# Dilated sliding attention into a gated unit: q and k loaded for two batches in full tiles, stores in pairs from another queue

## The chip, the cores and the metric

The kernel runs on one core of a Trainium2 chip. Its engines work side by side, each through its own list of instructions, and wait for each other by semaphores: TensorE (PE in the profile; PEld is its loading of weights) multiplies into PSUM, a memory of 8 banks; VectorE (DVE) and ScalarE (ACT) read and write PSUM and the on-chip memory SBUF; GpSimd (POOL) works on SBUF alone; SyncE (SP) only issues transfers. Transfers (DMAs) are moved by 16 DMA engines that all queues share. An engine that issues a transfer does so in its place in its own list. The metric is the device time of one execution in microseconds (us), as the median of the runs.

## The reference

Eight batches, eight heads, 576 positions, 64 values per head; all inputs are float32. Each head attends to 32 earlier positions: heads 0 to 3 to the last 32 in a row ("plain"), heads 4 to 7 to every fourth of the last 128 ("dilated"). The heads' outputs, side by side, are the x of a gated unit: a causal depthwise convolution of 5 taps and a sigmoid make the gate, x @ w_val the value, and their product goes through w_out.

```python
scores = scale * np.matmul(q, k.transpose(0, 1, 3, 2))
mask_plain = (rel >= 0) & (rel < window)                                   # window 32
mask_dil = (rel >= 0) & (rel < window * dilation) & (rel % dilation == 0)  # dilation 4
masks = [mask_plain if h < H // 2 else mask_dil for h in range(H)]
attn = softmax(np.where(masks, scores, -1e9))
x = np.matmul(attn, v)                      # then (B, S, H * D)
gate_pre[s] = sum(conv_w[j] * x[s - 4 + j] for j in range(5))
out = (sigmoid(gate_pre) * (x @ w_val)) @ w_out
```

## The kernel before, in words

The unit of attention work is an "attend": two neighbouring heads of one batch, 32 in all, four per batch (`order`, line 209). Of the group numbers g, 0 and 1 are plain and 2 and 3 dilated.

**Loads** (`load`, line 304), all issued by SP. q and k of an attend are one tile each of 96 partitions and 768 float32 (288 KB): dilated, 12 positions per partition, both heads one after the other; plain, 6 positions of each head side by side. v comes as two tiles of 96 and 80 partitions when dilated (lines 330, 332) and as three transfers when plain (lines 335 and 339), in blocks of 128 positions that overlap. Six buffers of q and of k, four of plain v and three of dilated v let loads run ahead.

**One attend** (`attend`, line 472). Plain q and k are first cast to bf16 on GpSimd (lines 486, 489); dilated ones are read as the upper halves of float32. TensorE transposes six slices of 96 partitions each (lines 351 and 356, with an identity as the moving operand), and ScalarE or VectorE copies the 576 columns out of PSUM to qT and kT (lines 362 and 364). Scores are computed in two halves (line 400), each followed by an exp on ScalarE (line 403). VectorE multiplies by a mask of zeros and ones (line 408). TensorE multiplies with v and a column of ones (lines 417, 427, 431), VectorE takes the reciprocal of the sums and scales (lines 436 and 437), TensorE transposes back (lines 454 and 458), and the result is copied to xT (362 or 364), which holds all eight batches.

**The gated unit** (`gated`, line 590) of a batch follows its four attends: for each of four chunks of 128 channels 20 convolution matmuls on halves of the array (line 547), a tanh on ScalarE (line 599, a sigmoid up to scale), eight value matmuls (line 557, which need all four attends' xT), and one VectorE instruction that forms y (line 603). Then come four output tiles of 128 positions, four matmuls each (line 565), copied out by ScalarE or VectorE (lines 570 and 572). Each is stored at once by SP (line 617, 256 KB). The last 32 positions of each half, of four batches together, make two more tiles after batches 3 and 7, stored by line 624. A second copy of w_val and w_out with head halves swapped serves the second half of the positions.

**The order** of every engine's list is worked out by a planner ahead of the run (`Plan`, lines 34 to 126). A task has dependencies, a cost on each engine that could do it, a priority and the PSUM banks it needs. The planner steps through a modelled time, takes the task that could start earliest (among close ones, the one of lowest priority number), and assigns its engine and banks. Its model lets at most eight transfers be in flight when SP issues one (`FLIGHT`), and runs all transfers one after the other:

```python
dma_free = max(dma_free, est + c + 1.3) + nbytes / rate
t.end = dma_free + 0.5
```

The planned order is then emitted, and semaphores keep the data right, however far the chip is from the model. Stores and loads share SP's list, so a store whose tile is not ready holds the loads behind it.

Of the kernel before, what the change touches and what calls it, by code (L numbers as in the profile page):

```python
# [33 lines left out]
class Plan:  # L34
# [6 lines left out]
    FLIGHT = 8  # L41

# [8 lines left out]
    def run(self):  # L51
        for t in self.tasks:
            t.deps = [d() if callable(d) else d for d in t.deps]
            t.deps = [d for d in t.deps if d is not None]
        free = {e: 0.9 for e in self.OVER}
# [6 lines left out]
        while todo:  # L62
            best = {}
            for t in todo:
                ready = 0.0
                for d in t.deps:
# [3 lines left out]
                    ready = max(ready, d.end + self.SYNC[src])  # L70
# [37 lines left out]
            if t.lag:  # L108
                free[e] = est + c
                nbytes, rate = t.lag  # L110
                dma_free = max(dma_free, est + c + 1.3) + nbytes / rate
                t.end = dma_free + 0.5
                flight.append(t.end)
            else:
                t.end = est + c
                free[e] = t.end - self.OVER[e]
# [13 lines left out]
def kernel(  # L130
# [10 lines left out]
    nc = tc.nc  # L141
# [32 lines left out]
    NQ, NV, NET, NX, NO = 6, 4, 3, 3, 6  # L174
    NY = 3
    qs = bufs(NQ, [96, 2 * S * D // 96], FP32, "q")
    ks = bufs(NQ, [96, 2 * S * D // 96], FP32, "k")
    vps = bufs(NV, [128, NB, 2, DA], FP32, "vp")
    vas = bufs(3, [96, 2, R * D], FP32, "va")
    vzs = bufs(3, [80, 2, R * D], FP32, "vz")  # L180
    vd0 = bufs(3, [96, 2, R, DA], BF16, "vda")
    vd1 = bufs(3, [80, 2, R, DA], BF16, "vdb")
    qcs = bufs(3, [96, 6, 2, D], BF16, "qc")
    kcs = bufs(3, [96, 6, 2, D], BF16, "kc")
    qTs = bufs(3, [128, S], BF16, "qT")
    kTp = bufs(3, [128, 32 + S], BF16, "kTp")
    kTd = bufs(3, [128, 640], BF16, "kTd")
# [5 lines left out]
    osbs = bufs(NO, [128, Dm], FP32, "osb")  # L193
    xT = consts.tile([128, NCH, B * SB], BF16, name="xT")
# [14 lines left out]
    order = [(b, g) for b in range(B) for g in ((2, 0, 3, 1) if b == 0 else (0, 2, 1, 3))]  # L209
# [7 lines left out]
    nth = {}  # L217
    seen = {True: 0, False: 0}
    for i in range(N):
        nth[i] = seen[is_dil(i)]  # L220
        seen[is_dil(i)] += 1
# [19 lines left out]
    def c_mask_p():  # L241
        band(mask_p[:, 0:96].rearrange("p (j t) -> p j t", j=6), 32, [[1, 6], [6, 16]], 1)
# [10 lines left out]

    def c_ident2():
# [4 lines left out]
    def c_kd():  # L259
        for x in kTd:  # L260
            nc.vector.memset(x[:, S:640], 0.0)
# [4 lines left out]

    def c_kp():
        for x in kTp:
            nc.vector.memset(x[:, 0:32], 0.0)
# [5 lines left out]
    def c_vp():  # L275
        for x in vps:
            nc.gpsimd.memset(x[:, :, :, D:DA], 1.0 - 2.0 ** -9)
            nc.gpsimd.memset(x[0:32, 0, :, :], 0.0)

    def c_xpad():  # L280
        nc.vector.memset(xT.rearrange("z c (b t) -> z c b t", b=B, t=SB)[:, :, :, 0:4], 0.0)
# [4 lines left out]
    K_kp = add("kp", -7, {"DVE": 0.2}, lambda t: c_kp())  # L286
# [6 lines left out]
    K_sp = add("sp", -5, {"DVE": 1.2}, lambda t: spread(mask_p, 12), [K_mp])  # L293
# [3 lines left out]
    LD = {}  # L297
    PAIR = {}

    def ld(name, i, nbytes, rate, emit, deps):  # L300
        t = add(name, i, {"SP": 0.45}, emit, list(deps), lag=(nbytes, rate))
        return t

    def load(i):
        b, g = order[i]
        dil = is_dil(i)
        def was(m, nm):
            return lambda: PAIR.get(m, {}).get(nm)

        qt, kt = qs[i % NQ], ks[i % NQ]  # L310
        P = PAIR[i] = {}
        for nm, dst, src, dep in (("q", qt, q, was(i - NQ, "rq")), ("k", kt, k, was(i - NQ, "rk"))):
            two = src[b, 2 * g:2 * g + 2]
            if dil:
                s = two.rearrange("h (p r) d -> (h p) (r d)", r=12)
                d = dst
            else:
                s = two.rearrange("h (p r) d -> p h (r d)", r=6)
                d = dst.rearrange("p (h c) -> p h c", h=2)
# [386 lines left out]
```

## Time and profile before

| | |
|---|---|
| median of 3 runs | 277.98 us (276.61 to 279.22) |
| the profiled execution | 276.3 us, of which its span (first to last instruction) is 274.3 |
| mean granted TensorE clock | 0.869 |
| busy: TensorE, VectorE, ScalarE, GpSimd | 190.6, 120.7, 118.4, 58.3 us |
| moved by DMA | 42.09 MB, 153 GB/s over the span |
| loads of q and k | 64 of 288 KB, 6.6 and 7.0 us to landing (median) |
| stores | 36 of 256 KB, 2.1 us to landing (median) |

How to read the profile: "busy" is the time in which an engine executes, as a share of the span in brackets. "40 slices" cuts the span into equal pieces; each digit is the busy share in tenths. "The chain that ended last" goes back from the last instruction, step by step, to what released it, and gives each engine's and line's share; a long wait that is not on it costs nothing. A row of a group reads: line, engine, operation, output<-input, count, busy time and mean of one, and after the bar the idle time before it with the releaser. A row of waits reads: who waited, for whom, total us, times, longest. A row of the timeline begins with its start and length in us. A row of a stretch gives its limits and length, the busy time of TensorE, its weight loads, VectorE, ScalarE and GpSimd with counts, then the clock, the DMA share (in sums of overlapping transfers it can pass 1) and GB/s.

### The profile page before, as it was taken

What the parts mean: (1) busy time and instruction counts of PE and PEld (TensorE: products, weight loads), DVE (VectorE), ACT (ScalarE), POOL (GpSimd) and SP (SyncE); (2) the same over time, 40 slices, a digit from 0 to 9 for tenths busy, and PEclk for the clock granted to TensorE, in tenths of its full rate; (3) what the DMA queues carried; (4) which work ended last, traced back from release to release, by engine and by line L of the source; (5) the groups of instructions that cost most, each with busy time, mean ns of one, the idle gap of its engine ahead of it and who ended that gap; (6) DMA issues with size and microseconds to landing.
All of it is one profiled execution on the core that took longest, in us unless ns stands there. A gap on an engine that the chain in (4) does not pass through costs nothing.

```text
span 274.3 us, 6193 instructions
## 1 busy us (share of the span) xinstructions
PE 190.6 (69%) x2548; PEld 131.0 (48%) x2548; DVE 120.7 (44%) x213; ACT 118.4 (43%) x196; POOL 58.3 (21%) x104
## 2 busy tenths in 40 slices
PE   3667567858678658587585778787887577677860
PEld 2556444544454446345454535555665345544520
DVE  5645444524445423514624355454674334535400
ACT  3453313652464551055430446455844352663150
POOL 6453210404021310070040510034050600100000
PEclk9999999977997955959759579999779799979995
DMA  7999991195974599305899017788999240003041
GB/s 194 244 238 259 252 217 39 51 247 146 240 137 148 163 245 234 66 0 167 217 224 182 3 38 213 212 215 271 236 217 224 54 155 0 26 17 115 2 158 71
DMA packets 47093, 42.09 MB, mean 153 GB/s; under 512 B 26453, under 2 KB 39253, under 8 KB 47066
## 3 DMA queue, kind: packets, MB, share of 16 engines
q1 hardware_dynamic: 46000, 40.64, 61.0%
q0 software_dynamic: 1056, 1.05, 2.3%
q8 instruction: 20, 0.33, 0.5%
q14 instruction: 7, 0.06, 0.1%
q10 hardware_dynamic: 10, 0.01, 0.0%
HBM read 32.78 MB, written 9.44 MB: 154 GB/s over the span
## 4 chain that ended last, share of the span: by engine, by line
PE 55%; DVE 20%; ACT 15%; issue 4%; DMA 2%; SPq 1%; POOL 0%; ACTq 0%; DVEq 0%
PE ps L557 13%; PE ps L565 11%; PE ps L547 10%; ACT et L403 8%; DVE xn L437 6%; DVE y L603 6%; PE ps L400 5%; PE ps L351 3%; ACT gate L599 3%; PE ps L356 3%; PE ps L417 3%; DVE xm L437 3%; DVE rec L436 2%; PE ps L454 2%; DMA q<-in_q_dram 2%
## 5 line engine op out<-in xcount | busy, mean ns | idle before, releaser
L403 ACT ACTIVATE et<-ps 128x576 bf16<-128x576 f32 x64 | 39.9, 650 | 38.8 <-PE ps L400 17.1
L557 PE MATMUL ps<-xT,w_val 128*128 128x288 bf16 x256 | 42.5, 317 | 7.3 <-DVE xn L437 2.5
L565 PE MATMUL ps<-w_out,y 128*128 128x512 bf16 x128 | 38.5, 438 | 3.5 <-DVE xm L437 1.2
L547 PE MATMUL ps<-xT,conv_d 64*64 64x288 bf16 x640 | 34.1, 344 | 8.1 <-ACT et L403 5.8
L603 DVE SCALAR_TENSOR_TENSOR y<-gate,ps 128x576 bf16<-128x576 bf16 x32 | 23.8, 752 | 30.1 <-PE ps L557 19.9
L557 PEld LDWEIGHTS <-w_val 128*128 128x128 bf16 x256 | 26.4, 108 | 18.4 <-issue 10.0
L570 ACT ACTIVATE osb<-ps 128x512 f32<-128x512 f32 x34 | 20.3, 597 | 23.5 <-PE ps L565 22.9
L599 ACT ACTIVATE gate<-ps 128x576 bf16<-128x576 f32 x32 | 20.6, 652 | 22.1 <-PE ps L547 10.4
L436 DVE RECIPROCAL rec<-ps 96x8 f32<-96x8 f32 (+1 forms) x48 | 10.0, 209 | 45.2 <-ACT gate L599 6.9
L547 PEld LDWEIGHTS <-conv_d 64*64 64x64 bf16 x640 | 21.5, 125 | 13.6 <-issue 9.3
L609 POOL COPY y_rem<-y 128x256 bf16<-128x256 bf16 x8 | 3.6, 456 | 110.8 <-DVE y L603 108.4
L437 DVE TENSOR_TENSOR xn<-ps,rec 96x512 bf16<-96x512 f32 (+1 forms) x32 | 26.2, 820 | 1.1
L516 POOL CAST vda<-va 96x512 bf16<-96x512 f32 x16 | 11.4, 710 | 57.1 <-DMA va<-in_v_dram 52.4
L565 PEld LDWEIGHTS <-y 128*128 128x128 bf16 x128 | 12.4, 108 | 18.8 <-issue 10.8
L362 ACT COPY xT<-ps 128x576 bf16<-128x576 bf16 x20 | 12.8, 639 | 19.3 <-PE ps L458 15.6
L408 DVE TENSOR_TENSOR et<-et,mask_p 128x1152 bf16<-128x1152 bf16 x16 | 13.4, 840 | 17.4 <-ACT et L403 17.4
L362 ACT COPY qT<-ps 128x576 bf16<-128x576 bf16 x19 | 12.2, 642 | 17.1 <-DVE xm L437 5.8
L364 DVE COPY xT<-ps 128x576 bf16<-128x576 bf16 x12 | 9.1, 757 | 18.5 <-PE ps L454 8.5
L489 POOL CAST kc<-k 96x768 bf16<-96x768 f32 x16 | 13.8, 861 | 15.7 <-DMA k<-in_k_dram 15.6
L408 DVE TENSOR_TENSOR et<-et,mask_d 128x1152 bf16<-128x1152 bf16 x15 | 12.5, 836 | 9.2 <-ACT et L403 9.2
L400 PE MATMUL ps<-qT,kTd 64*128 64x96 bf16 (+1 forms) x256 | 10.0, 209 | 9.0 <-DVE xn L437 2.7
L400 PE MATMUL ps<-qT,kTp 64*128 64x96 bf16 x192 | 9.6, 234 | 8.2 <-DVE xn L437 4.6
(67 smaller groups left out, 242.1 us busy)
## 6 DMA issues: line engine op xcount, KB each, us to landing
q<-in_q_dram SPq DMA_DIRECT2D x32, 288.0 KB, 6.6
k<-in_k_dram SPq DMA_DIRECT2D x32, 288.0 KB, 7.0
out_dram<-osb SPq DMA_DIRECT2D x36, 256.0 KB, 2.1
vp<-in_v_dram SPq DMA_DIRECT2D x32, 160.0 KB, 6.8
va<-in_v_dram SPq DMA_DIRECT2D x16, 192.0 KB, 5.8
vz<-in_v_dram SPq DMA_DIRECT2D x16, 160.0 KB, 7.3
vp<-in_v_dram SPq DMA_DIRECT2D x16, 48.0 KB, 7.0
w_val<-in_moe_w_val_dram POOLq DMA_DIRECT2D x1, 512.0 KB, 11.2
```

The lines of the kernel that those rows point to most:

```text
L362: nc.scalar.copy(out=out_, in_=in_)
L400: nc.tensor.matmul(out=o, lhsT=l, rhs=r, start=True, stop=True)
L403: nc.scalar.activation(out=et[:, hf * 576:hf * 576 + 576].rearrange("p (b c) -> p b c", b=2), in_=ps[:, :, 0:HALF], func=AF.Exp, scale=scale)
L408: eng.tensor_tensor(out=et[:, 0:ET], in0=et[:, 0:ET], in1=(mask_d if is_dil(i) else mask_p)[:, 0:ET], op=ALU.mult)
L436: nc.vector.reciprocal(out=rec[:, :, 0:n], in_=av[:, :, :, D])
L437: nc.vector.tensor_tensor(out=xo, in0=av[:, :, :, 0:D], in1=rec[:, :, 0:n, None].to_broadcast([96, 2, n, D]), op=ALU.mult)
L547: nc.tensor.matmul(out=ps[ob:ob + D, half, 0:HALF], lhsT=conv_d[x * D:x * D + D, c, kk, :], rhs=xT[x * D:x * D + D, c, s:s + HALF], start= ...
L557: nc.tensor.matmul(out=ps[:, half, 0:HALF], lhsT=w_val[half][:, mc, c * 128:(c + 1) * 128], rhs=xT[:, mc, s:s + HALF], start=(mc == 0), st ...
L565: nc.tensor.matmul(out=ps[:, :], lhsT=cols(c), rhs=w_out[half][:, c, :], start=(c == 0), stop=(c == NCH - 1))
L570: nc.scalar.activation(out=osb, in_=ps, func=AF.Copy, scale=0.5)
L599: th = add("tanh", base + 1.0 + 0.5 * c, {"ACT": 0.66}, lambda t, cv=cv, gt=gt: nc.scalar.activation(out=gt, in_=banks(cv, 2)[:, :, 0:HALF ...
L603: y = add("y", base + 1.2 + 0.5 * c, {"DVE": 0.76}, lambda t, c=c, vl=vl, gt=gt: nc.vector.scalar_tensor_tensor(out=y_all[:, c, b % NY, :] ...
```

## The change

*q and k.* Two batches form a pair. The 384 partition rows of one kind (plain or dilated), of q or k, are cut into three tiles u = 0, 1, 2 of 128 partitions (`rows`, `unit`). Tile 0 lies in the first batch and tile 2 in the second; tile 1 takes its first 64 rows from one and its last 64 from the other, which its DRAM pattern writes as a leading dimension of 2. Plain heads are now paired 0 with 2 and 1 with 3, so that 128 partitions hold two heads side by side; tile 1 of the plain kind is loaded in two pieces, one per head of the pair. `prepare` casts, transposes (128 columns a slice) and copies out 768 columns to a qT and kT that span both batches. An attend waits for the tiles that it needs: in the first batch, tile 0, and for its second attend of a kind also tile 1; in the second, tiles 1 and 2, and then tile 2.

*Stores.* Two output tiles share one buffer and go out in one transfer of 512 KB, issued by ScalarE; the two remainder tiles are evicted into one buffer and stored by two transfers, also from ScalarE.

*Weights.* With the new pairing, rows and columns of w_val, conv_w and w_out are put in order by three transfers in place of one, and both copies of w_val are formed by eight copies from a raw one that is held in w_out's second buffer until then.

*Planner and buffers.* Every dependency gets 0.1 us of slack; a task that needs a PSUM bank also waits, in the plan, for what the task that frees the bank waits for; the value matmuls wait for the convolution of their chunk; transfers from queues other than SP's are modelled otherwise; many rates and costs are changed. Batches take groups 2, 0, 3, 1 in turn. Buffers: three plain and two dilated v, two y, five batches of xT, four double output tiles. The plain mask has a first block of its own, and kT no leading zeros.

```diff
+    SLACK = 0.1
...
+        for t in self.tasks:
+            for u in t.frees:
+                u.deps += [d for d in t.deps if d not in t.frees and not d.frees]
...
-                    ready = max(ready, d.end + self.SYNC[src])
+                    ready = max(ready, d.end + self.SYNC[src] + self.SLACK)
...
-                dma_free = max(dma_free, est + c + 1.3) + nbytes / rate
-                t.end = dma_free + 0.5
+                if e == "SP":
+                    dma_free = max(dma_free, est + c + 1.3) + nbytes / rate
+                    t.end = dma_free + 0.5
+                else:
+                    dma_free = max(dma_free, est + c) + nbytes / rate
+                    t.end = est + c + 1.8 + 2 * nbytes / rate
                 flight.append(t.end)
...
-    NQ, NV, NET, NX, NO = 6, 4, 3, 3, 6
-    NY = 3
-    qs = bufs(NQ, [96, 2 * S * D // 96], FP32, "q")
-    ks = bufs(NQ, [96, 2 * S * D // 96], FP32, "k")
+    NQ, NV, NVD, NET, NX, NO, NY, NXT = 6, 3, 2, 3, 3, 4, 2, 5
+    G = 2 * NG * (S // 12)
+    qs = bufs(NQ, [128, 768], FP32, "q")
+    ks = bufs(NQ, [128, 768], FP32, "k")
...
-    vas = bufs(3, [96, 2, R * D], FP32, "va")
-    vzs = bufs(3, [80, 2, R * D], FP32, "vz")
...
-    qTs = bufs(3, [128, S], BF16, "qT")
-    kTp = bufs(3, [128, 32 + S], BF16, "kTp")
-    kTd = bufs(3, [128, 640], BF16, "kTd")
+    vas = bufs(NVD, [96, 2, R * D], FP32, "va")
+    vzs = bufs(NVD, [80, 2, R * D], FP32, "vz")
+    qcs = bufs(2, [128, 6, 2, D], BF16, "qc")
+    kcs = bufs(2, [128, 6, 2, D], BF16, "kc")
+    qTs = {kind: bufs(2, [128, 6, G], BF16, "qT" + kind) for kind in "dp"}
+    kTs = {kind: bufs(2, [128, 6 * G + 64 * (kind == "d")], BF16, "kT" + kind) for kind in "dp"}
...
-    osbs = bufs(NO, [128, Dm], FP32, "osb")
-    xT = consts.tile([128, NCH, B * SB], BF16, name="xT")
+    osbs = bufs(NO, [128, 2, Dm], FP32, "osb")
+    xT = consts.tile([128, NCH, NXT * SB], BF16, name="xT")
...
-    order = [(b, g) for b in range(B) for g in ((2, 0, 3, 1) if b == 0 else (0, 2, 1, 3))]
+    order = [(b, g) for b in range(B) for g in (2, 0, 3, 1)]
...
+    def heads(i):
+        b, g = order[i]
+        return (2 * g, 2 * g + 1) if is_dil(i) else (g, g + 2)
...
+    def rows(kind, u):
+
+        r = 12 if kind == "d" else 6
+        if u == 0:
+            part, off = [[r * D, 128]], 0
+        elif u == 1:
+            step = H * S * D - 128 * r * D
+            part, off = [[step, 2], [r * D, 64]], 128 * r * D
+        else:
+            part, off = [[r * D, 128]], H * S * D + 64 * r * D
+        width = r * D
+        if kind == "d":
+            return [(0, width, off, part + [[1, width]])]
+        if u == 1:
+            return [(x * width, width, off + x * 2 * S * D, part + [[1, width]]) for x in range(2)]
+        return [(0, 2 * width, off, part + [[2 * S * D, 2], [1, width]])]
+
+    def load_rows(src, kind, n, u, piece, dst):
+        o, w, off, ap = piece
+        base = src.offset + (2 * n * H + (NG if kind == "d" else 0)) * S * D
+        nc.sync.dma_start(out=dst[:, o:o + w], in_=bass.AP(tensor=src.tensor, offset=base + off, ap=ap))
+
+    def unit(n, kind):
+        for u in range(3):
+            first = 8 * n + (0, 2, 4)[u] + (kind == "p")
+            for w, (nm, ring, src) in enumerate((("q", qs, q), ("k", ks, k))):
+                m = SEQ.index((n, kind, u))
+                dst = ring[m % NQ]
+                before = SEQ[m - NQ] if m >= NQ else None
+                UNIT[n, kind, u, nm] = {}
+                UNIT[n, kind, u, nm]["buf"] = dst
+                pieces = rows(kind, u)
+                UNIT[n, kind, u, nm]["ld"] = [ld(
+                    "ld" + nm, first + 0.1 * w, 393.0 / len(pieces), 330.0,
+                    lambda t, dst=dst, src=src, u=u, piece=piece: load_rows(src, kind, n, u, piece, dst),
+                    [lambda before=before, nm=nm: UNIT[before + (nm,)]["free"] if before else None])
+                    for piece in pieces]
+
+    SEQ = [(n, kind, u) for n in range(B // 2) for u in range(3) for kind in "dp"]
...
+    def prepare(n, kind, u):
+
+        prio = 8 * n + (0, 2, 4)[u] + (kind == "p")
+        for nm in "qk":
+            U = UNIT[n, kind, u, nm]
+            src, got = U["buf"], U["ld"]
+            dst = (qTs if nm == "q" else kTs)[kind][n % 2]
+            m = SEQ.index((n, kind, u)) // 2
+            if kind == "p":
+                c = (qcs if nm == "q" else kcs)[m % 2]
+                before = SEQ[2 * (m - 2) + 1] if m >= 2 else None
+                raw = src
+                got = U["cast"] = add("cast", prio - 0.3, {"POOL": 0.87}, lambda t, raw=raw, c=c: nc.gpsimd.tensor_copy(
+                    c.rearrange("p j h d -> p h j d"), raw.rearrange("p (h j d) -> p h j d", h=2, j=6)),
+                    got + [UNIT[before + (nm,)]["tr"] if before else None])
+                got = [got]
+                U["free"] = U["cast"]
+                src = c
+            tr = U["tr"] = add("tr", prio - 0.05, {"PE": 0.34}, lambda t, src=src: transpose_in(t, kind, src),
+                               got + [K_ident], banks=1, mode="full")
+            if kind == "d":
+                U["free"] = tr
+            old = [PAIR[i]["sc"] for i in range(8 * (n - 2), 8 * (n - 1)) if is_dil(i) == (kind == "d")] if n >= 2 else []
+            if nm == "q":
+                U["ev"] = add("evq", prio - 0.04, {"DVE": 0.56, "ACT": 0.81}, lambda t, tr=tr, dst=dst: copy(
+                    t, dst[:, :, 128 * u:128 * u + 128], bank(tr, BF16)[:, 0:768].rearrange("p (f g) -> p f g", f=6)),
+                    [tr] + old, frees=[tr])
+            else:
+                U["ev"] = add("evk", prio - 0.04, {"ACT": 0.81, "DVE": 0.96}, lambda t, tr=tr, dst=dst: evict_k(
+                    t, kind, bank(tr, BF16), dst, u), [tr, K_kd] + old, frees=[tr])
...
+        b, g = order[i]
+        kind = "d" if dil else "p"
+        n = b // 2
+        if dil:
+            need = {(0, 2): (0,), (0, 3): (0, 1), (1, 2): (1, 2), (1, 3): (2,)}[b % 2, g]
+        else:
+            need = {(0, 0): (0,), (0, 1): (0, 1), (1, 0): (1, 2), (1, 1): (2,)}[b % 2, g]
+        ready = [UNIT[n, kind, u, nm]["ev"] for u in need for nm in "qk"]
+        qT, kT = qTs[kind][n % 2], kTs[kind][n % 2]
...
+    def out_tiles(prio, tiles, store):
...
-        sts = [add("st", prio, {"SP": 0.45}, lambda t, e=e: e(osb), [oe], lag=(nb, 340.0)) for e, nb in store]
...
+        oes, ots = [], []
+        for x, (half, cols, deps) in enumerate(tiles):
+            ot = add("ot", prio + 0.5 * x, {"PE": 0.87}, lambda t, half=half, cols=cols: outp(t, half, cols),
+                     list(deps) + K_wo[half], banks=1, mode="full")
+            oes.append(add("oe", prio + 0.5 * x, {"ACT": 0.60, "DVE": 0.69}, lambda t, x=x, ot=ot: evict_o(t, bank(ot), osb[:, x, :]),
+                           [ot] + (out_st[n - NO] if n >= NO else []), frees=[ot]))
+            ots.append(ot)
+        out_st.append([add("st", prio + 0.5, {"ACT": 0.40}, lambda t, e=e: e(osb), oes, lag=(nb, 340.0)) for e, nb in store])
+        return ots
...
-            for n in range(2):
-                t0 = half * HALF + n * 128
-                YO[b].append(out_tile(base + 3.2 + 0.5 * (2 * half + n), half,
-                         lambda c, t0=t0: y_all[:, c, b % NY, t0:t0 + 128], ys,
-                         [(lambda osb, t0=t0: nc.sync.dma_start(out=out[b, t0:t0 + 128, :], in_=osb), 262.0)]))
+            t0 = half * HALF
+            YO[b] += out_tiles(base + 3.2 + half, [
+                (half, lambda c, o=t0 + 128 * n: y_all[:, c, b % NY, o:o + 128], ys) for n in range(2)],
+                [(lambda osb, t0=t0: nc.scalar.dma_start(
+                    out=out[b, t0:t0 + 256, :].rearrange("(n p) d -> p n d", n=2), in_=osb), 524.0)])
...
     def load_w(t, dst, src):
-        nc.gpsimd.dma_start(out=dst, in_=src.rearrange("(c p) n -> p c n", p=128))
-
-    def swap_val(t):
-        wv = [w.rearrange("p m (c x d) -> p (m c) x d", x=2, d=D) for w in w_val]
+        cut = CH * 128
+        top = src[0:cut].rearrange("(x c d) n -> x d c n", x=2, c=CH)
         for x in range(2):
-            copy(t, wv[1][:, :, x, :], wv[0][:, :, 1 - x, :])
+            nc.gpsimd.dma_start(out=dst[x * D:x * D + D, 0:CH, :], in_=top[x])
+        nc.gpsimd.dma_start(out=dst[:, CH:, :], in_=src[cut:].rearrange("(c p) n -> p c n", p=128))
+
+    def order_val(t, half, part):
+        cut = CH * 128
+        raw = w_out[1]
+        lo, hi, src = ((0, cut, "p m (x c d) -> p m x c d"), (cut, Dm, "p m (c x d) -> p m x c d"))[part]
+        kw = {"x": 2, "d": D}
+        dv = w_val[half][:, :, lo:hi].rearrange("p m (c x d) -> p m x c d", **kw)
+        sv = raw[:, :, lo:hi].rearrange(src, **kw)
...
+    wv = add("ldwv", 1.0, {"POOL": 2.6}, lambda t: load_w(t, w_out[1], moe_w_val),
+             [UNIT[0, "p", 1, "q"]["ld"][0]], lag=(1049.0, 330.0))
+    K_wv = [add("ordv", 3.0 + half, {"DVE": 0.8, "ACT": 1.2}, lambda t, half=half, part=part: order_val(t, half, part),
+                [wv]) for half in range(2) for part in range(2)]
+    wo = add("ldwo", 5.0, {"POOL": 2.6}, lambda t: load_w(t, w_out[0], moe_w_out),
+             [PAIR[4]["lv"][0]], lag=(1049.0, 330.0))
+    so = [add("swo", 6.0, {"SP": 0.45}, lambda t, x=x: swap_out(t, x), [wo] + K_wv, lag=(262.0, 300.0)) for x in range(2)]
```

## The prediction

> **What bounds the kernel now.** I read the page first: busy times, the slices, the chain that ended last. In the fence: busy time by engine, the DMA row of the slices, and the chain by engine and by line.
>
> ```profile
> PE 190.6 (69%) x2548; PEld 131.0 (48%) x2548; DVE 120.7 (44%) x213; ACT 118.4 (43%) x196; POOL 58.3 (21%) x104
> ...
> DMA  7999991195974599305899017788999240003041
> ...
> PE 55%; DVE 20%; ACT 15%; issue 4%; DMA 2%; SPq 1%; POOL 0%; ACTq 0%; DVEq 0%
> PE ps L557 13%; PE ps L565 11%; PE ps L547 10%; ACT et L403 8%; DVE xn L437 6%; DVE y L603 6%; PE ps L400 5%; PE ps L351 3%; ACT gate L599 3%; PE ps L356 3%; PE ps L417 3%; DVE xm L437 3%; DVE rec L436 2%; PE ps L454 2%; DMA q<-in_q_dram 2%
> ```
>
> No engine is full. The chain hops between TensorE, VectorE and ScalarE; DMA is 2% of it, one load at the start. The slices say where that could change: the DMA engines are full for the first 39 us, then have gaps. So the second view is the busy time by stretch for 8 to 39 us, and the third the DMA alone in the kernel's last 5 us, when TensorE is done.
>
> ```profile
> 8.00:39.00 31.00, 20.74 (x288) 16.59 (x289) 15.96 (x27) 11.83 (x20) 11.45 (x14) 1.00 1.17 242
> ```
> ```profile
> 264.75 1.41 SPq L624 DMA_DIRECT2D out_dram<-osb  x2
> ```
> ```profile
> DMA  1131410222222232222223131322223132222312
> ...
> DMA packets 232, 0.46 MB, mean 93 GB/s; under 512 B 5, under 2 KB 5, under 8 KB 232
> ...
> q1 hardware_dynamic: 232, 0.46, 25.4%
> ```
>
> The last columns of the first fence are clock, DMA share and GB/s: 242 GB/s with the engines saturated, 15.1 GB/s for each of 16. The next fence, from the timeline, shows the two remainder stores (line 624) issued together, and the last is the DMA view from 267.5 to 272.5 us: their 256 KB each are still moving, with 25.4% of 16 engines busy, 4.06 engines, at 93/4.06 = 22.9 GB/s each. Their address pattern in DRAM starts with a dimension of 4 (four batches). The 2.1 us stores and the other loads start with 80, 96 or 128 rows. I read: **the leading dimension of the address pattern limits how many engines a transfer gets**, and two such transfers share the same ones, since two in flight hold four and not eight.
>
> Fourth, the first batch in the timeline and in the chain in order of time:
>
> ```profile
> 22.04 0.82 POOL L489 CAST kc<-k 96x768 bf16<-96x768 f32 x1 [0.48 <-DMA k<-in_k_dram]
> ```
> ```profile
> 39.03 2.08 PE ps L557 x8
> ...
> 254.09 2.73 PE ps L557 x21
> ```
>
> The k of attend 3, the last head pair of batch 0, is cast at 22.0; batch 0's first value matmul runs at 39.0, 17 us later, batch 7's at 254.1. So a batch takes 215.1/7 = 30.7 us, two batches 61.5, and from batch 7's first value matmul to the end it is 20.2 us. Last, the waits of SP's queue:
>
> ```profile
> SPq L617 <- ACT osb L570: 125.6, 28, 17.2
> SPq L321 <- DMA k<-in_k_dram: 8.5, 11, 1.1
> ```
>
> SP stands 125.6 us at stores whose tile is not evicted yet, with loads queued behind; and loads wait for earlier loads to land, so only a few may be in flight (the planner's FLIGHT says 8).
>
> **The change, part by part.** The sum is made on the profiled execution: 276.3 us, of which 274.3 are its span and 2.0 lie around it. It is 1.7 under the median of 277.98, and I add that at the end.
>
> *The middle tile of each triple.* Two batches' q of one kind are three tiles of 128 rows. The first and last lie in one batch. The second takes 64 rows of each, and its pattern starts with `[step, 2]`. By the remainder stores' row it runs on two engines, always the same two. Bounds: sixteen engines (a load may not follow the rule that a store follows) to two; I take two, the only row with a small leading dimension. Each such tile is 393,216 B, 196,608 per engine: 8.6 us at the 22.9 of the tail, 13.0 at the 15.1 of the saturated stretch. I take 8.6, since the other fourteen engines will mostly stand idle, as in the tail. q and k of both kinds: 34.3 us per pair of batches on those two engines (ends 34.3 and 52.1).
>
> Everything else is spread over sixteen: 42.09 MB, less 16 x 0.393 = 6.29 for the middle tiles, plus 0.26 for the plain v's wider first block (64 for 48 KB), 36.06 MB, 2.25 per engine. At 22.9 that is 98 us, at 15.1 149; I take 20 GB/s, nearer the tail's row: 113, or 28.2 per pair. The remainder stores stay on four engines, these two among them: 0.197 MB more than their even share, 8.6 us, 2.1 per pair. Sum **64.6 us per pair** (60.9 to 91).
>
> The Trainium skill, "DMA: Bandwidth & Descriptors", section "Why a DMA increments its semaphore by 16 and not by 1", speaks against this change: the engine count is the largest number up to 16 that divides the slowest dimension of both sides, and the lowest-numbered engines are taken. The four-engine tail agrees; which engines they are no view here names. By its other rule, in "Rules for kernel authors" (128 partitions for bandwidth), the tiles would gain and the sum would be the fast rival's 271.
>
> *Start.* Ahead of the last middle tile, in the planner's priority order, go four u=0 tiles (98 KB per engine) and the v of attends 0 to 2 (70 KB): 168 KB at the start's 15.1, 11.1 us. With 2.5 us to the first data and 34.3, k for attend 3 is ready at 48 in place of 22, 26 us late. From that cast to batch 0's last xT copy was 12 us (33.43 to 34.2), so its value matmuls can't start before 60: 21 late. Between, some conv and the next pair's transposes can be brought forward, but the next tiles stand behind in the same queues. I take **+17** (12 to 26).
>
> *After the start.* The engines' 64.6 stands against compute's 61.5, less 1.8 from the savings below, 59.7: 4.9 late per pair, three more pairs, **+15** (+4 to +94). The loads may run a pair ahead (six buffers), which makes the queue continuous but adds no rate. The waits come where there are none now: transposes and casts on q and k, with exps and masks behind them.
>
> *Transposes.* 64 groups of six become 48, on 128 columns. A group takes 0.66 us; as long each would save 16 x 0.66 = 10.6, as long per column nothing. Lines 351 and 356 are 6% of the chain, 17 us; a quarter is 4. I take -3 (0 to -10.6).
>
> *Evictions of q and k.* ScalarE's 576 columns take 650 ns (line 403), its 512 take 597 (line 570): 0.83 ns per column, so 768 cost about 0.81 us as an estimate. 48 x 0.81 = 38.9 for 64 x 0.65 = 41.6: -2 (0 to -2.7).
>
> *Casts* on POOL: 32 of 0.82 to 0.86 become 24 of the same free size. POOL is busy 21%: nothing; if POOL should come late, -7.
>
> *Stores to ScalarE's queue.* Of the 36 stores of 256 KB, 32 become 16 double ones and the four remainders stay four; all move. An issue took 0.36 (line 617) to 0.56 us (line 624) on SP: 20 of them, 7 to 11 us of ScalarE. ScalarE is 43% busy and 15% of the chain: +2 (0 to +11). Queued behind a waiting store are the exps, for which masks and the second matmuls wait; a store waits for both tiles' evictions and for its DMA slot. SP's 125.6 us go, but the chain has no load behind them: nothing on today's path.
>
> *Weights.* Three issues each for one, on POOL's queue (0.75 to 0.93 us each), and eight reordering copies for two of 0.73, some 3 us on DVE or ScalarE, begun after the middle plain tile's first half. They lie beside the late start: nothing; without it, +4. The w_out swap waits for these copies on SP with loads behind it, again beside the full engines. Masks, fewer buffers, head order: nothing, since the rings hold two or more still; up to 5 us if a two-deep v or y ring comes late.
>
> *The new order.* No row prices it. "issue" is 4% of the chain, 11 us: bounds -11 and +11; I take -4, because the slack removes some waits of one engine for another's last few tens of ns. Savings: 3 + 2 + 4 - 2 = 7.
>
> Sum: 276.3 + 17 + 15 - 7 = 301.3; with the 1.7, **303 us**.
>
> **Rivals.** *A, 303 (0.50, own range 288 to 325):* the two engines pace the loads. *B, slower still, 335 (0.20, 315 to 400):* at the contended rate a pair costs 91 us, 31 more than compute, 95 in all and 18 more at the start: 303 + 80 + 18 = 401 at the far end. Less far: a store on ScalarE waits for the slot of a load that queues behind middle tiles, half of 34 us in two of the four pairs, +34. For it: the rings are shared and loads already wait for loads; against it: the two engines mostly run alone.
>
> *C, faster, 271 (0.15, 260 to 275):* the loads spread over sixteen engines after all. Then start and later lateness both go: 276.3 - 7 + 1.7. For it: only stores show the limit. It decides if the middle tiles land in the 6.6 to 7 us of today's q and k. *D, hidden, 279 (0.15, 275 to 288):* two engines, but the rest goes at 22.9, a pair costs 60.9 and is covered, and half the start is filled with other work: 276.3 + 8 - 7 + 1.7. For it: the clock was 0.67 from 100 to 120 us, so a TensorE that pauses may be granted more afterwards.
>
> **How the numbers follow.** 303 is A's. From 270 to 340 lie A and D whole, half of C and over half of B, some 0.85. A measurement of this kernel tells about 1% from no change: faster is C but for its top and a little of D, 0.15; within 1% the rest of C and half of D, 0.08; slower 0.77.
>
> **What would show it.** Middle loads that land in 15 us or more, DMA shares near 2/16 (0.12) for long stretches with some 45 GB/s; k casts of attend 3 at 45 to 50 us; the first value matmul near 56 to 60; DMA of 10% or more on the chain. Wrong if the middle loads run at 200 GB/s, if batch 0's value matmuls start by 42, or if the new order alone gains over 20 us. B shows as exps idle behind a store on ScalarE's queue for 10 us or more.

## The result, and the profile after

The changed kernel takes 361.3 us (359.9 to 364.2) against 278.5 before: 1.300 times as long, 95% interval 1.289 to 1.311. The forecast was 303 in a range of 270 to 340: the sign was right and the size was not. (Some executions of a kernel run longer at a lower granted clock; the ratios given compare the others.) The page of its profiled execution, whose span is 358.8 us: busy times, the clock and DMA rows of the slices, the chain.

```profile
PE 208.7 (58%) x2452; PEld 140.9 (39%) x2452; DVE 129.2 (36%) x221; ACT 110.1 (31%) x174; POOL 57.5 (16%) x98
...
PEclk9999999978556868655955989886576599766997
DMA  7225399921169146321277029222139421100331
...
PE 41%; DMA 14%; DVE 14%; ACT 11%; SPq 11%; issue 4%; POOL 1%; ACTq 1%; DVEq 0%; POOLq 0%
DMA k<-in_k_dram 11%; PE ps L601 11%; PE ps L609 10%; PE ps L591 7%; SPq L331 7%; ACT et L463 6%; DVE xn L497 5%; DVE y L652 5%; PE ps L384 5%; ACT gate L648 3%; SPq L371 3%; PE ps L460 3%; DVE rec L496 2%; PE ps L477 2%; DMA va<-in_v_dram 2%
```

DMA and SP's queue, 3% of the chain before, are 25% now, 90 us, and the row of the slices has long runs of 1 and 2 where it had nines. One such run, the DMA view from 88 to 93 us:

```profile
DMA  1111011111111111111111111111111111111111
...
DMA packets 174, 0.24 MB, mean 48 GB/s; under 512 B 6, under 2 KB 170, under 8 KB 174
...
q1 hardware_dynamic: 174, 0.24, 13.2%
```

13.2% of 16 is 2.1 engines, 48 GB/s, 23 for each: the middle tiles run on two engines at the rate taken from the remainder stores (22.9). Here is the chain in order of time, first at the start, then at the largest later stall (start, length, what):

```profile
27.95 18.34 DMA k<-in_k_dram
46.30 0.02 issue
46.32 0.02 POOLq L414
46.34 0.08 issue
46.42 0.84 POOL kc L414
...
86.61 15.38 DMA k<-in_k_dram
101.99 0.02 issue
102.01 0.02 ACTq L666
102.03 0.04 issue
102.06 0.45 ACTq L666
...
103.31 1.21 ACT gate L648 x2
```

At the start the k of attend 3 is cast at 46.4 in place of 22.0. At 87 us something else happens: a landing k load releases line 666, which is a *store*. Nothing in the data joins the two. The timeline of ScalarE at that place:

```profile
82.61 0.64 ACT L388 COPY xT<-ps 128x576 bf16<-128x576 bf16 x1 [0.52 <-PE ps L514]
102.06 0.45 ACTq L666 DMA_DIRECT2D out_dram<-osb  x1
102.61 0.80 ACT L388 COPY qTd<-ps 128x768 bf16<-128x768 bf16 x1 [19.36 <-DMA k<-in_k_dram]
103.31 1.20 ACT L648 ACTIVATE gate<-ps 128x576 bf16<-128x576 f32 x2
```

ScalarE's list stands still for 19 us with the store at its head, tanh and exps behind it. The tile was evicted at 82.1. Two more such stops, of 10.5 and 8.0 us ahead of an osb copy, stand in ScalarE's waits (total, times, longest), and shorter ones of 2.7 and 2.8 follow them:

```profile
ACT osb L614 <- DMA vp<-in_v_dram: 18.5, 2, 10.5
```

To part the stretches I take the last VectorE y of the first and of the last batch (end of its row in the timeline), which split an execution into start, seven batches, and tail:

| profiled execution | first batch done | seven more batches | tail to the end |
|---|---|---|---|
| before | 49.4 | 210.1 | 14.8 |
| after | 71.7 | 271.8 | 15.3 |
| leading 128 (below) | 51.0 | 230.9 | 15.3 |
| stores on GpSimd (below) | 74.6 | 226.6 | 16.6 |
| halves (below) | 55.8 | 213.6 | 15.2 |
| halves, stores planned for and issued by SP (below) | 55.7 | 201.3 | 14.8 |
| leading 2, stores planned for and issued by SP (below) | 74.9 | 230.7 | 14.9 |
| before, with heads two apart (below) | 70.6 | 225.0 | 14.9 |

Of the 84.5 us by which the span grew, 22.3 lie in the start and 61.7 in the seven batches after it.

### The profile page after: what moved, and what is told of

It is laid out like the page before. It is cut to its first block, busy times and chain, and to the rows that moved or that the text cites. A ratio compares the mean times of both kernels' runs of the same rounds, so it can differ in the third digit from the quotient of the medians.

```text
span 358.8 us, 5844 instructions
## 1 busy us (share of the span) xinstructions
PE 208.7 (58%) x2452; PEld 140.9 (39%) x2452; DVE 129.2 (36%) x221; ACT 110.1 (31%) x174; POOL 57.5 (16%) x98
## 4 chain that ended last, share of the span: by engine, by line
PE 41%; DMA 14%; DVE 14%; ACT 11%; SPq 11%; issue 4%; POOL 1%; ACTq 1%; DVEq 0%; POOLq 0%
DMA k<-in_k_dram 11%; PE ps L601 11%; PE ps L609 10%; PE ps L591 7%; SPq L331 7%; ACT et L463 6%; DVE xn L497 5%; DVE y L652 5%; PE ps L384 5%; ACT gate L648 3%; SPq L371 3%; PE ps L460 3%; DVE rec L496 2%; PE ps L477 2%; DMA va<-in_v_dram 2%
## 5 line engine op out<-in xcount | busy, mean ns | idle before, releaser
L601 PE MATMUL ps<-xT,w_val 128*128 128x288 bf16 x256 | 48.9, 352 | 11.6 <-ACT et L463 4.8
L591 PE MATMUL ps<-xT,conv_d 64*64 64x288 bf16 x640 | 37.2, 377 | 20.3 <-ACT osb L614 12.6
L601 PEld LDWEIGHTS <-w_val 128*128 128x128 bf16 x256 | 29.1, 118 | 25.9 <-issue 11.8
L591 PEld LDWEIGHTS <-conv_d 64*64 64x64 bf16 x640 | 23.4, 136 | 27.3 <-issue 22.6
L496 DVE RECIPROCAL rec<-ps 96x8 f32<-96x8 f32 (+1 forms) x48 | 10.1, 210 | 62.6 <-ACT et L463 23.7
L390 DVE COPY xT<-ps 128x576 bf16<-128x576 bf16 x15 | 11.4, 757 | 51.9 <-ACT gate L648 18.5
L460 PE MATMUL ps<-qTd,kTd 64*128 64x96 bf16 (+1 forms) x256 | 10.8, 223 | 29.4 <-ACT gate L648 22.3
L388 ACT COPY xT<-ps 128x576 bf16<-128x576 bf16 x17 | 10.9, 639 | 41.2 <-DVE y L652 16.7
L460 PEld LDWEIGHTS <-kTd 64*128 64x128 bf16 x256 | 8.3, 111 | 34.1 <-issue 31.2
L468 DVE TENSOR_TENSOR et<-et,mask_d 128x1152 bf16<-128x1152 bf16 x15 | 12.4, 827 | 25.4 <-ACT et L463 25.4
L560 POOL CAST vda<-va 96x512 bf16<-96x512 f32 x16 | 10.6, 664 | 65.1 <-DMA va<-in_v_dram 32.1
L460 PE MATMUL ps<-qTp,kTp 64*128 64x96 bf16 x192 | 9.3, 226 | 9.7 <-DVE y L652 3.9
L384 PE MATMUL ps<-ident,qc 128*128 128x128 bf16 x72 | 7.8, 261 | 11.4 <-POOL qc L414 5.0
```

Source lines behind the costliest of these rows:

```text
L384: nc.tensor.transpose(out=ps[:, f * 128:f * 128 + 128], in_=lhs, identity=ident)
L460: nc.tensor.matmul(out=o, lhsT=l, rhs=r, start=True, stop=True)
L468: eng.tensor_tensor(out=et[:, 0:ET], in0=et[:, 0:ET], in1=(mask_d if is_dil(i) else mask_p)[:, 0:ET], op=ALU.mult)
L591: nc.tensor.matmul(out=ps[ob:ob + D, half, 0:HALF], lhsT=conv_d[x * D:x * D + D, c, kk, :], rhs=xT[x * D:x * D + D, c, s:s + HALF], start= ...
L601: nc.tensor.matmul(out=ps[:, half, 0:HALF], lhsT=w_val[half][:, mc, c * 128:(c + 1) * 128], rhs=xT[:, mc, s:s + HALF], start=(mc == 0), st ...
```

## The experiments

Theory T: the leading 2 confines these loads to two engines, and all of the loss follows from that. Rival P: the new order, the smaller rings or the stores on ScalarE cost the time themselves. Theory T2, from the profile after: past the start, the slow loads reach the chain only through the stores in ScalarE's list.

**The same bytes in one pattern of 128 rows.** Order and number of transfers stay as in the changed kernel.

```diff
-            step = H * S * D - 128 * r * D
-            part, off = [[step, 2], [r * D, 64]], 128 * r * D
+            part, off = [[r * D, 128]], 128 * r * D
```

> The changed kernel with only the DRAM pattern of the middle q and k tiles altered: a leading dimension of 128 in place of [step, 2], the same bytes, the same number of transfers, the same planned order. Left out of the computation: the second half of tile 1 holds rows that follow in the first batch, not those of the second. Theory T (the leading 2 confines these loads to two engines, and all of the loss comes from that, at the start and through the stores that wait behind them): 265 to 280 us, 0.73 to 0.78 of the changed kernel; middle tiles land in under 10 us; batch 0's first value matmul near 42 us in place of 62. Rival P (the new order, the smaller rings and the stores on ScalarE cost the time themselves): 320 us or more; the loads get faster and the stalls stay.

Measured: 295.4 us, 1.057 (1.052 to 1.063) of before. The pattern alone is worth 65.9 of the 82.8 us. DMA falls to 2% of the chain. The longest waits for a load are 4.1 us on TensorE, for the first q, and 5.4 on GpSimd, for a v; past 76 us no engine that computes waits for a load at all. But the time doesn't fall to 280: 17 us remain that have nothing to do with the pattern, so T explains most and not all. (The profiled execution of the table lies some 4 us above this kernel's median, so of its 20.8 us over the seven batches of before, some 17 are the usual.)

**Two halves of 64 partitions**, one from each batch, all of the computation done:

```diff
-            part, off = [[step, 2], [r * D, 64]], 128 * r * D
+            off = 128 * r * D
...
+        inner = [[1, width]] if kind == "d" else [[2 * S * D, 2], [1, width]]
         if u == 1:
-            return [(x * width, width, off + x * 2 * S * D, part + [[1, width]]) for x in range(2)]
+            return [(64 * y, 64, off + y * step, [[r * D, 64]] + inner) for y in range(2)]
...
-        nc.sync.dma_start(out=dst[:, o:o + w], in_=bass.AP(tensor=src.tensor, offset=base + off, ap=ap))
+        nc.sync.dma_start(out=dst[p:p + n_, :], in_=bass.AP(tensor=src.tensor, offset=base + off, ap=ap))
```

> The changed kernel with each middle tile of q and k loaded by two transfers of 64 partitions, one from each batch (leading dimension 64): dilated tiles take one transfer more than in the changed kernel, plain ones as many. The whole computation is done. Theory T: as the leading dimension of 128, within 2%, 265 to 280 us. Rival P: 320 us or more. If the number of transfers matters (eight in flight), up to 10 us more than with the leading 128.

Measured: 287.4, 1.029 (1.025 to 1.034). Eight more transfers did not cost; the kernel planned with them is 8 us faster than the run above, although the work is the same. Pattern and number of transfers differ too, so this is only a first hint of what the plan by itself can move.

**The stores issued by GpSimd**, with leading 2 and plan kept (the remainder stores likewise):

```diff
-                [(lambda osb, t0=t0: nc.scalar.dma_start(
+                [(lambda osb, t0=t0: nc.gpsimd.dma_start(
```

> The changed kernel, leading 2 and planned order kept, but the stores issued from GpSimd's queue, at the same place of the planned order, so that ScalarE waits for no transfer slot. Theory T2 (after the start the loss reaches the chain through ScalarE's stores, which wait for slots of loads behind the middle tiles: 19, 12 and 12 us in the profile after): 310 to 330 us. Rival A (the two engines' rate paces everything, whoever issues the stores): 350 us or more. GpSimd's casts may be held by the waiting stores instead, which would give back up to 20 us and land between.

Measured: 320.9, 1.150 (1.140 to 1.159): 40.5 us less than the changed kernel, as T2 said. ScalarE's timeline at the same place of the work:

```profile
85.85 0.64 ACT L388 COPY xT<-ps 128x576 bf16<-128x576 bf16 x1 [0.52 <-PE ps L514]
88.20 0.80 ACT L388 COPY qTd<-ps 128x768 bf16<-128x768 bf16 x1 [1.71 <-DVE xn L497]
89.02 0.65 ACT L648 ACTIVATE gate<-ps 128x576 bf16<-128x576 f32 x1
```

The 19.4 us stop before the copy to qTd is 1.7 us here, and it ends with VectorE, not with a load. The table says more: with its two engines as slow as ever, this kernel does the seven later batches in 226.6 us, no more than with the fast pattern (230.9, usually some 227). Past 76 us its casts of q and k wait 1.4 us in all for loads. So in this plan, past the start, the two engines alone cost nothing, and the rate argument of the forecast (64.6 us of load against 59.7 of compute per pair) found no place in the chain. The plan takes some 65 us per pair with fast loads too; what happens in a plan that leaves less room, two runs below show.

**The pattern in the kernel before**, first with the two neighbouring heads as the dimension of 2:

```diff
                 s = two.rearrange("h (p r) d -> (h p) (r d)", r=12)
+                if nth[i] % 3 != 2:
+                    s = bass.AP(tensor=src.tensor, offset=src.offset + (b * H + 2 * g) * S * D,
+                                ap=[[S * D, 2], [12 * D, 48], [1, 12 * D]])
```

> The kernel before, with the DRAM pattern of the q and k loads of 11 of its 16 dilated attends written with a leading dimension of 2 (one per head) in place of 96 rows: the same bytes to the same places, 22 loads of 0.295 MB, 6.49 MB in all against the change's 6.29. Theory T: the pattern alone makes the kernel before slow too: loads of 147 KB per engine at 22.9 GB/s take 6.4 us each, 141 us of two engines in all, the start is late by some 13 us, and stores and loads share SP's list: 310 to 370 us. Rival P: under 290, since order, rings and stores are as before. If the two merged strides are sent as one dimension, 278 and no sign of two engines; then the run tells nothing.

Measured: 278.2, the same as before; q and k land in 6.7 and 6.8 us as ever. The two strides make one run of 96 rows, so this run tells nothing on the theories, only that such a pattern is harmless. Then with heads two apart:

```diff
+                    s = bass.AP(tensor=src.tensor, offset=src.offset + (b * H + g + 2) * S * D,
+                                ap=[[2 * S * D, 2], [12 * D, 48], [1, 12 * D]])
```

> The kernel before, with q and k of 11 of its 16 dilated attends loaded by a pattern with a leading dimension of 2 that can't be merged into one: heads 4 and 6, or 5 and 7, two head strides apart. Left out: in these attends the q and k of one of the two heads are another head's; bytes, tiles and order are those of the kernel before. The earlier run with neighbouring heads showed the 6.7 us median landing of the kernel before, so its pattern was merged and it told nothing. Theory T: 22 loads of 147 KB per engine at 22.9 GB/s, 6.4 us each when alone: 141 us on two engines; first batch 10 to 15 us late, 300 to 350 us in all. Rival P: under 285.

Measured: 314.4, 1.124 (1.115 to 1.132). The pattern alone, in the old kernel with the old order and SP's stores, is enough to add some 34 us, by that ratio: in the profiled executions 21 in the start and 15 in the seven batches after it. The chain by line of its page:

```profile
DMA k<-in_k_dram 20%; PE ps L560 10%; PE ps L568 9%; PE ps L550 8%; ACT et L406 6%; DMA va<-in_v_dram 5%; DVE y L606 5%; DVE xn L440 5%; PE ps L403 3%; PE ps L354 3%; ACT gate L602 2%; PE ps L359 2%; PE ps L420 2%; SPq L342 2%; DVE rec L439 2%
```

A k load, not among the entries of the chain of the kernel before, is the first here. Two such loads, at 79 and 221 us, are on the chain past the start, for 15 and 17 us. Each releases the transposes of that k, with no store between, since no store is in ScalarE's list here.

**What is left: slack, rings, stores.** Three runs on the kernel with halves (287.4).

```diff
-    SLACK = 0.1
+    SLACK = 0.0
```

> The kernel with the middle tiles in two halves (287 us), with the planner's slack of 0.1 us per dependency taken out; the order is planned anew from that. Theory S (the slack in the plan is what makes the rest of the change slower than the kernel before): 278 us or less. Rival (the slack helps, as the prediction took it): 290 or more. Within 2 us of 287: the slack is not it.

Measured: 290.6, 1.046 (1.041 to 1.052). The slack is not the cause; without it the kernel is a little slower.

```diff
-    NQ, NV, NVD, NET, NX, NO, NY, NXT = 6, 3, 2, 3, 3, 4, 2, 5
+    NQ, NV, NVD, NET, NX, NO, NY, NXT = 6, 4, 3, 3, 3, 3, 3, 4
```

> The kernel with the middle tiles in two halves (287 us), with the rings of v and y as before (four plain and three dilated v, three y), for which the double output tiles go from four to three and xT from five batches to four. Theory B (shorter rings make loads and y late): 279 to 284 us. Rival: within 2 us of 287, or slower where the three output tiles or four xT come late.

Measured: 285.4 in two of four runs and 291.8 in the other two. The faster two are 2 us under the 287.4, so the rings are not the 14 us that the next run gains.

```diff
-        out_st.append([add("st", prio + 0.5, {"ACT": 0.40}, lambda t, e=e: e(osb), oes, lag=(nb, 340.0)) for e, nb in store])
+        out_st.append([add("st", prio + 0.5, {"SP": 0.45}, lambda t, e=e: e(osb), oes, lag=(nb, 340.0)) for e, nb in store])
...
-                [(lambda osb, t0=t0: nc.scalar.dma_start(
+                [(lambda osb, t0=t0: nc.sync.dma_start(
```

> The kernel with the middle tiles in two halves (287 us), with the stores back on SP's queue, still in pairs, and planned there. Theory Q (ScalarE's issues, 20 of 0.4 to 0.6 us, and their waits cost the remaining 8 us): 278 to 283 us. Rival (nothing on the chain waits for them once the loads are fast): 285 to 290. If SP's waiting stores hold the loads: over 290.

Measured: 273.0, 0.985 (0.978 to 0.991): 14 us less, and faster than before by 1 to 2%. But two things changed in this run, the engine that issues and the plan. The next two runs part them.

**Plan against queue.** Both edits are made on the kernel with halves. The first keeps its plan and lets SP issue the stores at the same place; the second plans as the 273 us kernel does and leaves the issue with ScalarE.

```diff
-                [(lambda osb, t0=t0: nc.scalar.dma_start(
+                [(lambda osb, t0=t0: nc.sync.dma_start(
```

```diff
-        out_st.append([add("st", prio + 0.5, {"ACT": 0.40}, lambda t, e=e: e(osb), oes, lag=(nb, 340.0)) for e, nb in store])
+        out_st.append([add("st", prio + 0.5, {"SP": 0.45}, lambda t, e=e: e(osb), oes, lag=(nb, 340.0)) for e, nb in store])
```

> The kernel with halves (287 us), its plan unchanged (stores planned on ScalarE), but each store issued by SP at the same place of the order. Theory Q (the issue and its waits in ScalarE's list cost the 14 us between 287 and 273): 275 us or less. Rival (the other plan that SP's stores lead to brings the 14 us): within 3 us of 287, or more where SP's loads now wait behind stores.

> Halves, with the plan that the planner makes for stores on SP (the 273 us kernel), but each store issued by ScalarE at its place of the order. Theory R (the plan is the difference of 14 us: with stores costed at 0.4 us on ScalarE it gives VectorE twelve more instructions, six of them k copies at 950 in place of 800 ns): 273 to 277 us. Theory Q (a store in ScalarE's list costs time by itself): 281 or more; here its waits are unplanned, which could add to it.

Measured: 288.1, 1.037 (1.028 to 1.045), and 272.0, 0.977 (0.966 to 0.988). The queue is worth nothing in either plan; the plan is worth 14 to 16 us. None of it lies in the start (55.8 and 55.7 us, both some 6 later than before); it lies in the seven batches after it (213.6 and 201.3). Part of what differs shows in the pages' busy times, first of the 287 us kernel, then of the 273 us one:

```profile
PE 190.6 (67%) x2440; PEld 132.7 (47%) x2452; DVE 126.1 (44%) x221; ACT 110.2 (39%) x174; POOL 56.9 (20%) x98
```
```profile
PE 187.4 (69%) x2452; PEld 128.8 (47%) x2452; DVE 115.6 (43%) x209; ACT 118.3 (44%) x186; POOL 58.7 (22%) x98
```

With stores costed on ScalarE, the planner gives VectorE twelve instructions more, 10.5 us of its time for 8.1 of ScalarE's; among them are six of its eight k copies, which take 950 ns there and 800 on ScalarE in the groups by shape. That this shift is what the 14 us come from, and not the order that goes with it, was not tried.

**The fourth cell**: leading 2 kept, stores planned on and issued by SP, that is, the change of the 273 us kernel on the changed kernel itself.

> The changed kernel with its leading 2 kept, but the stores planned on and issued by SP: the fourth cell beside 361 (leading 2, ScalarE), 287 (halves, ScalarE) and 273 (halves, SP). Theory T2 (slow loads and ScalarE's stores multiply: a store there waits for the slot of a slow load): 300 to 320 us, that is, the two engines cost 27 to 47 with SP's stores against 74 with ScalarE's. Rival A (the two engines cost 74 whoever stores): 345 us or more.

Measured: 321.9, 1.152 (1.141 to 1.163), just above what T2 expected. So two engines cost 74 us with stores planned and issued on ScalarE (361.3 to 287.4) and 49 without (321.9 to 273.0), the plans that go with them included. Of the 49, 19 lie in the start (74.9 for 55.7) and 29 in the seven batches after it (230.7 for 201.3), with no store in ScalarE's list. Past 60 us GpSimd's casts of q, k and v wait 86 us for loads, for 35 in the 273 us kernel. So T2's "only" holds for the plan of the changed kernel and not in general: in this faster plan the slow loads do reach the casts directly. They come late for two reasons that no run parts, the two engines and SP's list, which stands at stores that are not evicted (next to nothing is loaded from 74 to 85 us).

**The remainder stores**, on the 273 us kernel, one transfer of 32 rows per batch in place of four batches in one:

```diff
-                    out=out[b - 3:b + 1, half * HALF + 256:half * HALF + HALF, :], in_=osb[:, half, :]), 262.0)
-                 for half in range(2)])
+                    out=out[b - 3 + x, half * HALF + 256:half * HALF + HALF, :],
+                    in_=osb[32 * x:32 * x + 32, half, :]), 65.5)
+                 for half in range(2) for x in range(4)])
```

> Halves and SP's stores (273 us), with each of the four remainder stores cut into four of 64 KB, one per batch, so that the DRAM pattern's leading dimension is 32 in place of 4. Theory T (the leading dimension sets the number of engines for stores too): the last stores' DMA share rises from about 0.25 to near full, their 5 us shrink to under 2, and six more issues of some 0.4 us on SP at the end give part of it back: 269 to 272 us. Rival: no change in the share, 274 to 276 for the issues.

Measured: 269.0, 0.967 (0.961 to 0.973): the fastest version of this study, and 3.3% under the kernel before. The DMA view of its last 5 us:

```profile
DMA  9999999997348626924681595077300000000000
...
q1 hardware_dynamic: 491, 0.71, 50.9%
...
out_dram<-osb SPq DMA_DIRECT2D x6, 64.0 KB, 1.7
```

Where the two remainder stores held a quarter of the engines for 5 us, the eight small ones and the store before them use 50.9% on average, and the small ones land in 1.7 us. Their issue, one after the other, now takes 3.6 us, and the tail is 10.6 us for 14.8.

## Why the prediction was wrong

Step by step, in medians: all parts of the change but the two engines, +16.9 (278.6 to 295.4); the two engines, with stores off ScalarE, +25.4 (to 320.9); ScalarE's stores behind the slow loads, +40.5 (to 361.3).

*The middle tiles on two engines: right.* 8.6 us per tile was from 22.9 GB/s per engine; the profile after shows 2.1 engines at 23. The trace agrees with the Trainium skill's page "DMA: Bandwidth & Descriptors", section "Why a DMA increments its semaphore by 16 and not by 1" (the number of engines is the largest up to 16 that divides the slowest dimension of both sides), for dimensions of 2 and 4 and for loads and stores; that the lowest-numbered engines are taken no view here shows.

*Start, +17: the mechanism right, the size a little low.* k of attend 3 was forecast at 48 us and was cast at 46.4. The first batch was 22.3 us late, inside 12 to 26. Batch 0's first value matmul ran at 62.2 for 39.0, 23 us late, where the forecast worked out 21 at the least and took 17 for work brought forward; that work made up for none of it.

*After the start, +15: the step failed in this plan.* It said that the loads, running a pair ahead, keep the two engines' queue continuous and so pace everything at 64.6 us per pair. In the changed kernel the queue is not continuous: SP's list holds middle tiles behind v loads, and SP waits 66 us there for v buffers that TensorE frees (total, times, longest):

```profile
SPq L368 <- PE ps L477: 35.8, 3, 13.7
SPq L368 <- PE ps L460: 30.6, 2, 21.0
```

The last of these waits, some 11 us, comes after the last q and k. From 119 to 128 and from 200 to 212 us almost nothing is moved (1 GB/s). Nor does the rate set the pace: with GpSimd's stores the seven batches take 226.6 us for some 227 with the fast pattern. Where compute is faster, the step was not idle: the fourth cell adds 29 us after the start and takes 65.9 us per pair (230.7/3.5) for 57.5 (201.3/3.5). That is near the 64.6 and 59.7 of the forecast, but with the gaps that SP's stores make there, the agreement may be chance.

*Stores to ScalarE's queue, +2 (0 to +11): the step that failed most.* Its cost was taken from the issue, 0.36 to 0.56 us each, and the issue indeed costs nothing (288.1 for 287.4; 272.0 for 273.0). The wait for a transfer slot was named there and left without a price. It is 40.5 us, in stops of up to 19 us. The price stood in rival B, +34 for half of 34 us in two of the four pairs, with a chance of 0.20 and a range of its own, 315 to 400, that holds the result; the sum of A left it out. The two are one case: if the loads are as slow as A says, whoever waits for their slots waits as long.

*The new order, -4 (-11 to +11): wrong in sign.* Without the two engines the rest costs 9 to 17 us and not the 7 less of the sum. The order and engines chosen by the planner are what moves it: with the same tiles, transposes and copies, plans made for stores on SP take 272 to 273.

*Transposes, copies, casts, weights: not separated.* A copy of 768 columns took 800 ns on ScalarE, for the 810 worked out. All of them together, with the better plan, are worth -5 us (273.0 for 277.7). That this is close to the -3 and -2 of the sum shows nothing, since the plan is in it. Rings: nothing, as forecast.

*The rivals.* C, that loads spread over all engines, is refuted by the 13% share; D, that they hide, by 46.4. B's mechanism was the main one after the start: 40.5 us, for the 34 that it put on it.

## What to carry to other kernels

Read the leading dimension of every transfer's DRAM pattern: a stray 2 or 4 there, whose stride does not run on into the next one, leaves most DMA engines out, and the DMA share of a lone transfer shows it at once (0.13 and 0.25 here). What that costs depends on what waits behind it: 66 us here with stores in ScalarE's list, 25 with the same plan and the stores on GpSimd, 34 in the kernel before. An engine that issues a transfer can wait for a slot that an unrelated slow transfer holds; price that wait by the slowest transfer in flight, not by the issue. And where a planner assigns engines, a changed cost of one small task can move more than the task itself: compare plans with the queue kept, and queues with the plan kept.

## What the runs showed of the hardware that I had not expected

- A confined load holds up its issuer. SP's issue of a q load, 0.46 us in the median before, takes up to 6.1 us in the profile after while the two engines are behind, and that of a v load up to 10.1; in the same plan with the leading 128 it is 2.2 and 2.9 at most. The rows of SP's timeline at 157 and 162 us in the profile after, two issues each:

```profile
156.88 5.14 SPq L331 DMA_DIRECT2D q<-in_q_dram  x2
162.07 10.28 SPq L331 DMA_DIRECT2D k<-in_k_dram  x2
```

- A leading dimension of 2 whose stride continues the next one costs nothing (278.2 us); one that does not continue it costs some 34.
- The granted TensorE clock was 0.793 in the changed kernel for 0.869 before, 0.83 with the leading 128 and 0.89 to 0.90 in the versions under 274 us, each in its profiled execution; the value matmuls took 352 ns in place of 317 on average. With stores on GpSimd they took 356, though the mean clock was 0.861, so the one does not follow the other. The forecast's guess that a pausing TensorE may be granted more later was not borne out: the slices after the pause at 72 to 103 us show fives to eights. Whether the pauses lower the clock or the bursts between them was not tried.
